# One plan of 730 named units orders a chain of sparse attention, channel mix and gated dense attention

## The chip, the cores and the metric

The kernel runs on one core of a Trainium2 chip. The metric is the time of one execution in device microseconds (us); of several executions the median is taken. TensorE is called PE here, VectorE DVE, ScalarE ACT, GpSimd POOL and SyncE SP, as the profile names them.

## The reference

Three stages in a row, on a batch of 4 with 576 positions:

```python
# stage 1: q, k, v are (4, 8, 576, 64); heads 0-3 local, heads 4-7 strided
scores = scale * np.matmul(q, k.transpose(0, 1, 3, 2))
mask_local = (rel >= 0) & (rel < 32)
mask_strided = (rel >= 0) & (pos[None, :] % 32 == pos[:, None] % 32)
x = softmax(where(mask, scores)) @ v            # to (4, 576, 512)
# stage 2: x_prev is x moved by one position
xk = mu_k * x + (1.0 - mu_k) * x_prev
xr = mu_r * x + (1.0 - mu_r) * x_prev
k = np.maximum(xk @ w_k, 0.0)                   # 512 -> 1024
x = sigmoid(xr @ w_r) * (k * k @ w_v)
# stage 3: four experts of width 64, causal, the two best by x @ w_gate
for e in range(4):
    q, k, v = x @ wq[e], x @ wk[e], x @ wv[e]
    ye = softmax(causal(scale * (q @ k.transpose(0, 2, 1)))) @ v @ wo[e]
    out += weight_of_e_if_among_the_two_best * ye
```

wq and wk are scaled up by 200. In the kernel most matrices are split into a high and a low fp32r part, and a product is three matmuls (high by high, low by high, high by low).

## The kernel before, in words

The kernel does not write its instructions down in the order in which the engines run them. A `Recorder` (line 187) stands in for the engines. Each operation recorded gets a rank (`len(self.ops)` at that moment) and a cost for each engine that could do it; matmuls that follow each other in one tiling of the array form one operation, until `cut()` closes it. At the end `order()` (line 357) lays the operations out in a modelled time: among those that one engine could start within `NEAR` (0.10 us) of the earliest, it takes the one of lowest rank. A PE operation that would change the tiling of the array has `stay` added to its rank (15 in stages 1 and 2, 10 in stage 3). `copy` may run on ACT or DVE, whichever would end first; most copies out of PSUM are such. `warm()` (line 346) puts matmuls on a tile of zeros ahead of a PE operation where the model has a gap of over 0.35 us in the first 80. `give()` issues everything (line 452, which is therefore the line of nearly every row of the trace), and `pinned()` fixes the order of each engine.

So the order of recording is the plan. It has these parts:

- Stage 1 of a batch (`p1_units`): per pair of heads a load, then pieces (three local thirds or two strided groups). Each piece is scores (`sl` local, `ss` strided, two heads side by side on halves of the array), softmax (`el`, `es`, on DVE and ACT), transposes (`ptl`, `pts`), their copies (`aTl`, `aTs`), the product with v (`pol`, `pos`) and its copy into `xT`.
- Stage 2 (`p2_units`): chunks A (320 positions) and Z (256). `r` and `k` are the token shift, `g` the product with w_r (`pr`), `m` with w_k (`pk`, then relu and square), `v` with w_v (`pv`, times the sigmoid, stored to `x_spill`). In the first batch a few products run on unsplit inputs (`xw`).
- Weights of stage 2 come in pieces: a load into `wraw`, a high part (`w`), a low part (`P`). `w3_units` does it for stage 3.
- Stage 3: `proj_units` gives q, k (`pq_False`, `pq_True`), v and the gate (`pvv`). Half of each K is copied to the other 64 partitions, its high part KH and low part KL by a DMA each that POOL issues. `attn_tiles` gives, for each of five tiles of queries, scores (`s`), softmax, transposes (`pt`), value products (`py`, a small tiling: 64 columns of the array) and the output product (`pw`), with a copy to `ot` and a store.

Before, the plan is made by rules. `first_batch()` runs the strings of `PLAN`: a head, written by hand, for the beginning, and a list that `interleave()` mixes with stage 1 of batch 1 by costs and a lead (0.9). `in_order` and `interleave` mix stage 2 of one batch with stage 1 of the next (0.85). In stage 3 the tiles form a pipeline with lags: scores of tile i, transposes of i - 1, py of i - 2, pw of i - 3 at one step, mixed with the projections of the next batch (0.85).

```python
def interleave(main, side, rec=None, lead=1.0):
    tm = lead * sum(c for c, _ in main) or 1.0
...
        if is_ < len(side) and (im >= len(main) or as_ / ts_ <= am / tm):
...
for i in range(b * per, len(steps) + 3 * last):
    for lag in range(4):
        if 0 <= i - lag < len(steps):
```

Of the kernel before, what the change touches and what calls it, by code (L numbers as in the profile page):

```python
# [9 lines left out]
F32 = mybir.dt.float32  # L10
# [8 lines left out]
P = 128  # L19
BIG = 3.0e38  # L20
PLAN = (
    "L1q L0q ident L0v L1v S3 L2q L3q zero L3v L0 L1 L2v L0m L1m L2 L3 L4 L5 L6 L7 L8 L9 L10 L11 L12 S4 S0 L13 W1 S1 S6 L14 S7 L15 W2 S9 Ar0 S8 Ar1 W0 W5 Ar2 W3 S5 S2 Ag0 Ag1 Ar3 Zr0 Zr2 Ak0 W6 Ak1 L16 W7 Zr3 Ak3 W4 L17 Ag2 Ak2 Am0 W9 L18 Zr1 W15 W11 W8 Am1 Age W10 Am2 W12 W16",
    "W13 Zg1 Am3 W14 Am4 Zg0 Zg3 L19 Zg2 Am5 Am6 W17 Am7 P8 W19 P15 P2 W18 P14 Zk0 P12 sig P13 Av0 P7 P10 P19 P17 P16 P18 P11 P6 Av1 Av2 Zk1 Av3 Av4 Zk3 P4 Zk2 Av5 P5 Av6 P9 Zm0 Zm1 Zm2 Zm3 Zm4 Av7 P1 Zm5 Zm6 Zm7 Zv0 Zv1 Zv2 Zv3 Zv4 Zv5 P0 Zv6 Zv7 P3",
)
# [12 lines left out]

def interleave(main, side, rec=None, lead=1.0):

    tm = lead * sum(c for c, _ in main) or 1.0  # L40
    ts_ = sum(c for c, _ in side) or 1.0
    im = is_ = 0
    am = as_ = 0.0
    while im < len(main) or is_ < len(side):
        if is_ < len(side) and (im >= len(main) or as_ / ts_ <= am / tm):
            c, f = side[is_]
            if rec is not None:
                rec.cut()
            f()
            as_ += c  # L50
            is_ += 1
        else:
            c, f = main[im]
            if rec is not None:
                rec.cut()
            f()
            am += c
            im += 1
# [92 lines left out]
class LazyPool:  # L151
    def __init__(self, make, bufs, psum=False, after=()):
        self.make, self.bufs, self.psum, self.after = make, bufs, psum, after
        self.made, self.rows, self.left = None, {}, 0
# [6 lines left out]
    def tile(self, shape, dtype, tag=None, name=None, bufs=None, lane=None, most=0):  # L161
        t = LazyTile(self, list(shape), dtype, bufs, dict(tag=tag, name=name))
        t.lane, t.most = lane, most
        t.row = self.rows.setdefault(tag, Row())
        t.row.free = [0.0] * (bufs or self.bufs)
        t.row.append(t)
        cols = np.arange(t.width).reshape(shape[1:])
        return View(t, (), dtype, 0, shape[0], cols)


def dram_view(ap):

# [14 lines left out]
class Recorder:  # L187
# [8 lines left out]
    STAY = 0  # L196
# [4 lines left out]
    def __init__(self, nc):  # L201
        self.nc = nc
        self.ops, self.on, self.open, self.more = [], False, None, []
        for e in self.ENGINES:
            setattr(self, e, self._engine(e))
# [32 lines left out]

    def add(self, ways, a, k):
# [9 lines left out]
        if mode is None or op is None or op.mode != mode:  # L249
            op = Op()  # L250
            op.stay = self.STAY
# [105 lines left out]
    def order(self):  # L357
# [43 lines left out]
        while len(given) < len(ops):  # L401
# [55 lines left out]
def kernel(  # L457
# [39 lines left out]
    def lazy(stack, name, bufs, after=(), before=None, **kw):  # L497
# [4 lines left out]
        return LazyPool(make, bufs, psum="space" in kw, after=after)  # L502
# [39 lines left out]
    nc.STAY = STAY1  # L542

    nc.zeros = p1.tile([P, P], F32, tag="zeros", name="zeros", bufs=1)
    nc.zeros.at = 1.6
# [115 lines left out]
    def p1_units(b):  # L661
        units = []
        xT = p2.tile([P, NKC, S + 1], F32, tag="xT", name=f"xT{b}", bufs=2)
        xTs[b] = xT

        def zero():
            nc.gpsimd.memset(xT[:, :, 0:1], 0.0)

        units.append((0.1, zero))
# [7 lines left out]
        def pair(hp):  # L677
# [56 lines left out]
            loads.append([(0.1, load), (0.0, load_rest)] + [(0.0, load_more)] * (b == 0 and local))  # L734

            def local_third(hf):
# [38 lines left out]
                def av_f():  # L775
# [11 lines left out]
                    evac(xT[:, hp, 1 + n * hf:1 + n * hf + n], po[:, :n])  # L787

                return (0.9, 0.4, 0.6), (sc_f, ex_f, no_f, tr_f, av_f)

            def strided_group(gi):
# [35 lines left out]
                def av_f():  # L827
# [10 lines left out]
                    xv = xT[:, hp, 1:].rearrange("p (n s) -> p n s", s=32)[:, :, r0:r0 + ng * nr]  # L838
# [5 lines left out]
                return (1.2, 0.6, 0.9), (sc_f, ex_f, no_f, tr_f, av_f)  # L844
# [6 lines left out]
        if b == 0:  # L851
            return units, loads, [f for _, f in stages]
        stages = [
            ((cs, lambda f=f: (f[0](), f[1](), f[2]())), (ct, f[3]), (ca, f[4]))
            for (cs, ct, ca), f in stages
        ]
        units += loads[0] + loads[1]
        groups = ((0, 1, 2), (3, 4, 5), (6, 7), (8, 9))
        for g in range(len(groups) + 1):
            if g in (1, 2):  # L860
                units += loads[g + 1]
            for n, i in ((1, g - 1), (2, g - 1), (0, g)):
                if 0 <= i < len(groups):
                    part = [stages[j][n] for j in groups[i]]
                    units.append((sum(c for c, _ in part), lambda part=part: [f() for _, f in part]))
        return units

    def p2_units(b):
        xT = xTs[b]
        parts = []  # L870
        for ci, (s0, N) in enumerate(CHUNKS1):
            st = {}

            def prep(which, kc, ci=ci, s0=s0, N=N, st=st):
                def f():
# [8 lines left out]
                    cur = xT[:, kc, 1 + s0:1 + s0 + N]  # L884
                    prv = xT[:, kc, s0:s0 + N]
# [14 lines left out]
                return (0.0, f)  # L900
# [4 lines left out]
            def mm1(fc, ci=ci, N=N, st=st):  # L905
# [28 lines left out]
                return (1.5 * N / 288, f)  # L934
# [18 lines left out]
            def mm3(oc, ci=ci, s0=s0, N=N, st=st):  # L953
# [14 lines left out]
                return (1.5 * N / 288, f)  # L968
# [4 lines left out]
            def mm2(oc, ci=ci, s0=s0, N=N, st=st):  # L973
                def half(hf):
# [19 lines left out]
                    return (1.5 * N / 288, f)  # L994
# [5 lines left out]
    def in_order(parts):  # L1000
        A, Z = parts
        return A["r"] + A["k"] + A["3"] + Z["r"] + A["1"] + Z["k"] + Z["3"] + A["2"] + Z["1"] + Z["2"]
# [19 lines left out]
    def first_batch():  # L1022

        (zero,), loads, steps = p1_units(0)
        A, Z = p2_units(0)
        pieces = weight_pieces()
        every = range(NKC)

        nc.vector.memset(nc.zeros, 0.0)
        todo = {"ident": [lambda: nc.sync.dma_start(ident, c_ident)], "zero": [zero[1]]}  # L1030
        for hp, l in enumerate(loads):
            for n, (_, f) in zip("qvm", l):
                todo[f"L{hp}{n}"] = [f]
        for i, step in enumerate(steps):
            todo[f"S{i}"] = step
        for j, (l, w, p) in enumerate(pieces):
            todo[f"L{j}"], todo[f"W{j}"], todo[f"P{j}"] = [l], [w], [p]
        for n, U in (("A", A), ("Z", Z)):
            for kc in every:
                todo[f"{n}r{kc}"], todo[f"{n}k{kc}"] = [U["r"][kc][1]], [U["k"][kc][1]]  # L1040
            for fc in range(NFC):
                todo[f"{n}m{fc}"] = [U["1"][fc][1]]
            for i, (_, f) in enumerate(U["2"]):
                todo[f"{n}v{i}"] = [f]
        for n, kcs in enumerate(((0, 1), (2,), (3,))):
            todo[f"Ag{n}"] = [lambda oc=oc, kcs=kcs: A["g"](oc, kcs) for oc in every]
        todo["Age"] = [lambda oc=oc: A["ge"](oc) for oc in every]
        for oc in every:
            todo[f"Zg{oc}"] = [lambda oc=oc: Z["g"](oc, every), lambda oc=oc: Z["ge"](oc)]
        todo["sig"] = [lambda: nc.scalar.activation(sg, sg, AF.Sigmoid)]  # L1050

        def run(name):
            for f in todo[name]:
                nc.cut()
                f()

        head, rest = (p.split() for p in PLAN)
        for name in head:
            run(name)
        cost = {"A": 1.6, "Z": 1.3}  # L1060
        return [(cost[n[0]] if n[1] in "mv" and n[0] in cost else 0.5 if n[0] == "P" else 0.0, lambda n=n: run(n)) for n in rest]

    def mixed(units, others):
        res = []
        interleave([(1.0, lambda u=u: res.append(u)) for u in units], [(1.0, lambda u=u: res.append(u)) for u in others])
        return res
# [16 lines left out]
    def w3_units():  # L1083

        units = []
        for src, h, l in ((wq, wqh, wql), (wk, wkkh, wkkl), (wvg, wvgh, wvgl), (wo, woh, wol)):
# [8 lines left out]
            units.append((0.0, load))  # L1095
            for r in range(0, rows, rows // 2):
# [5 lines left out]
                units.append((1.0, part))  # L1102
        return units

    A, Z = p2_units(B - 1)
    main = in_order((A, Z))
    n = len(main) - len(A["2"] + Z["1"] + Z["2"])
    interleave(main[:n], [], nc)
    interleave(main[n:], w3_units(), nc)
# [3 lines left out]
    nc.sync.dma_start(mcau, c_cau)  # L1113

# [426 lines left out]
```

## Time and profile before

| what | us |
|---|---|
| median of 3 runs (lowest, highest) | 525.83 (524.87, 526.89) |
| the profiled execution | 525.04 |
| its span, first to last instruction | 523.3 |
| PE busy | 518.0 (99%), 4360 instructions |
| DVE busy | 367.3 (70%), 1318 instructions |
| ACT busy | 314.4 (60%), 929 instructions |
| mean granted clock of TensorE | 0.999 of full |

In a row of the timeline the first number is the start in the span, the second the time from there to the end of the row's last instruction. Matmuls overlap, so the price of one is read from start to start of neighbours, not from its duration. A matmul of plain float32 operands (not split ones) has two records in the trace, so counts there are twice those of the order. A row's brackets give the idle time ahead of it on its engine, and what ended it.

### The profile page before, as it was taken

What the parts mean: (1) busy time and instruction counts of PE and PEld (TensorE: products, weight loads), DVE (VectorE), ACT (ScalarE), POOL (GpSimd) and SP (SyncE); (2) the same over time, 40 slices, a digit from 0 to 9 for tenths busy, and PEclk for the clock granted to TensorE, in tenths of its full rate; (3) what the DMA queues carried; (4) which work ended last, traced back from release to release, by engine and by line L of the source; (5) the groups of instructions that cost most, each with busy time, mean ns of one, the idle gap of its engine ahead of it and who ended that gap; (6) DMA issues with size and microseconds to landing.
All of it is one profiled execution on the core that took longest, in us unless ns stands there. A gap on an engine that the chain in (4) does not pass through costs nothing.

```text
span 523.3 us, 11666 instructions
## 1 busy us (share of the span) xinstructions
PE 518.0 (99%) x4360; PEld 483.1 (92%) x4360; DVE 367.3 (70%) x1318; ACT 314.4 (60%) x929; POOL 37.8 (7%) x88
## 2 busy tenths in 40 slices
PE   9999999999999999999999999999999999999997
PEld 8767799999999999999999999999999998998886
DVE  3999999639773758674747733266999768766991
ACT  4999985727673825664734553144765555666664
POOL 0000000000000000000000000033232030211000
PEclk9999999999999999999999999999999999999999
DMA  8997022221203330203021230055233330312112
GB/s 263 366 414 292 1 96 85 105 63 71 72 1 110 106 122 11 73 2 108 14 61 61 83 112 30 31 144 131 63 95 78 106 90 3 90 32 67 51 43 90
DMA packets 28892, 50.22 MB, mean 96 GB/s; under 512 B 4900, under 2 KB 23332, under 8 KB 28068
## 3 DMA queue, kind: packets, MB, share of 16 engines
q1 hardware_dynamic: 23716, 44.76, 25.0%
q0 software_dynamic: 5120, 4.72, 4.4%
q8 instruction: 34, 0.56, 0.4%
q14 instruction: 22, 0.18, 0.1%
HBM read 35.18 MB, written 9.44 MB: 85 GB/s over the span
## 4 chain that ended last, share of the span: by engine, by line
PE 96%; DVE 2%; ACT 0%; issue 0%; ACTq 0%
PE pk L452 20%; PE pv L452 20%; PE pr L452 10%; PE s L452 6%; PE pvv L452 5%; PE pw L452 5%; PE pq_False L452 5%; PE pq_True L452 5%; PE pt L452 5%; PE py L452 5%; PE sl L452 3%; PE pol L452 2%; PE ss L452 2%; PE ptl L452 2%; PE pos L452 1%; PE pts L452 1%
## 5 line engine op out<-in xcount | busy, mean ns | idle before, releaser
L452 PE MATMUL pv<-kk,wvh 128*128 128x320 f32 (+1 forms) x512 | 104.0, 297 | 0.0
L452 PEld LDWEIGHTS pv<-kk,wvh 128*128 128x128 f32 x512 | 81.2, 188 | 1.1
L452 PE MATMUL pk<-xh,wkh 128*128 128x256 f32 (+1 forms) x224 | 67.3, 300 | 0.0
L452 PE MATMUL pk<-xl,wkh 128*128 128x256 f32 (+1 forms) x224 | 65.3, 292 | 0.0
L452 ACT ACTIVATE rf<-pk 128x320 f32<-128x320 f32 (+1 forms) x64 | 25.5, 406 | 42.2 <-PE pk L452 41.8
L452 ACT ACTIVATE pe<-pe,nm 128x384 f32<-128x384 f32 (+4 forms) x72 | 41.8, 583 | 14.2 <-DVE nm L452 12.2
L452 DVE TENSOR_TENSOR sg<-pv,sg 128x320 f32<-128x320 f32 (+1 forms) x32 | 14.6, 456 | 42.2 <-PE pv L452 41.9
L452 PEld LDWEIGHTS pk<-xh,wkh 128*128 128x128 f32 x224 | 42.1, 188 | 1.1
L452 PEld LDWEIGHTS pk<-xl,wkh 128*128 128x128 f32 x224 | 42.1, 188 | 0.0
L452 DVE CUSTOM_DVE_ANT_0 pe<-s,mcau 128x384 f32<-128x384 f32 (+4 forms) x72 | 32.6, 483 | 6.4 <-PE s L452 6.1
L452 ACT ACTIVATE es<-es,nm 108x108 f32<-108x108 f32 (+1 forms) x80 | 30.4, 383 | 5.3 <-DVE nm L452 5.1
L452 ACT ACTIVATE el<-el,nm 128x96 f32<-128x96 f32 x72 | 26.1, 364 | 6.6 <-DVE nm L452 6.2
L452 DVE CAST kk<-rf 128x320 fp32r<-128x320 f32 (+1 forms) x51 | 15.7, 309 | 20.2 <-ACT rf L452 19.9
L452 DVE TENSOR_TENSOR kk<-rf,kk 128x320 fp32r<-128x320 f32 (+1 forms) x64 | 28.8, 456 | 1.6 <-ACT kk L452 0.4
L452 PE MATMUL pt<-ident,pe 128*128 128x128 f32 x200 | 29.8, 276 | 0.0
L452 ACT ACTIVATE rf<-rf 128x320 f32<-128x320 f32 (+1 forms) x64 | 28.0, 445 | 1.2
L452 PE MATMUL pr<-xh,wrh 128*128 128x320 f32 (+1 forms) x96 | 28.7, 299 | 0.0
L452 PE MATMUL pr<-xl,wrh 128*128 128x320 f32 (+1 forms) x96 | 28.2, 294 | 0.0
L452 DVE SCALAR_TENSOR_TENSOR xf<-xd,mu,xT 128x256 f32<-128x256 f32 (+1 forms) x52 | 25.7, 510 | 0.2
L452 DVE TENSOR_SCALAR pe<-pe,sm 128x384 f32<-128x384 f32 (+4 forms) x72 | 25.2, 397 | 0.4
L452 PEld LDWEIGHTS pt<-ident,pe 128*128 128x128 f32 x200 | 23.0, 140 | 2.2 <-ACT aT L452 0.3
L452 PE MATMUL py<-aT,V 128*64 128x320 f32 (+4 forms) x224 | 24.6, 362 | 0.0
(291 smaller groups left out, 1562.2 us busy)
## 6 DMA issues: line engine op xcount, KB each, us to landing
qkv<-in_loc_dram SPq DMA_DIRECT2D x6, 1168.0 KB, 5.4
qkv<-in_strd_dram SPq DMA_DIRECT2D x6, 896.0 KB, 4.9
wraw<-in_w_k_dram SPq DMA_DIRECT2D x8, 512.0 KB, 9.8
wraw<-in_w_v_dram SPq DMA_DIRECT2D x8, 512.0 KB, 10.2
x_spill<-sg SPq DMA_DIRECT2D x16, 160.0 KB, 1.7
x2f<-x_spill SPq DMA_DIRECT2D x4, 640.0 KB, 4.6
out_dram<-ot SPq DMA_DIRECT2D x16, 160.0 KB, 1.8
wraw<-in_w_r_dram SPq DMA_DIRECT2D x4, 512.0 KB, 7.5
```

Of the source, the lines that this page charges most:

```text
L452: f[o.engine](*[now(x) for x in a], **{n: now(x) for n, x in k.items()})
```

## The change

`PLAN` is one string of 730 names. The digit is the batch. In stage 1, `L` is a load (`q`, `v`, `m` its parts), `S` scores and softmax of a piece, `T` its transposes, `V` its product with v. `L`, `W`, `P` with a number are also pieces of the weights in the first batch. `A` and `Z` with `r`, `k`, `g`, `m`, `v` are stage 2. `u`, `x`, `k`, `q`, `v`, `t`, `g`, `n` are the projections of stage 3, `s` scores, `m` the norm, `p` transposes, `a` the value products, `o` the output products. `Recorder.unit` takes a unit's name and function, `Recorder.run` records the units as the plan names them; `interleave`, `first_batch`, `in_order` and the lags are gone. The ordering of the recorded operations (`order()`) stays, but for constants of its model: when zeros are there, and how DMAs of SP land. Batches 2 and 3 of stages 1 and 2 stand nearly in the regular order of before; the first batch (with batch 1 and a part of 2 among it) and stage 3 are reshuffled. The tile `xT` of a batch is made in its unit `z`.

```diff
-PLAN = (
-    "L1q L0q ident L0v L1v S3 L2q L3q zero L3v L0 L1 L2v L0m L1m L2 L3 L4 L5 L6 L7 L8 L9 L10 L11 L12 S4 S0 L13 W1 S1 S6 L14 S7 L15 W2 S9 Ar0 S8 Ar1 W0 W5 Ar2 W3 S5 S2 Ag0 Ag1 Ar3 Zr0 Zr2 Ak0 W6 Ak1 L16 W7 Zr3 Ak3 W4 L17
...
+PLAN = """
+0L1q 0z 0L0q 0i 0L2q 0L1v 0S3 0L0 0S4 0T3 0V3 0L3q 0L3v 0L1 0L0v 0L0m 0L2v 0S1 0L1m 0W1 0W0 0T4 0S0 0L2 0S6 0T1 0L3
...
+3a10 3p12 3a11 3a00 3a01 3o11 3o13 3o03 3o00 3o12 3o10 3o01 3o02
+"""
...
-LATE = True
-STAY3 = 10
...
-STAY1 = 15
-LEAD0 = 0.9
-LEAD1 = 0.85
-LEAD2 = 0.85
...
+    def unit(self, name, f):
+
+        assert name not in self.units, name
+        self.units[name] = f, self.stay
+
+    def run(self, plan):
+        for self.token in plan.split():
+            f, self.stay = self.units.pop(self.token)
+            self.cut()
+            f()
+        assert not self.units, self.units
...
-                link = max(link, s + (1.6 if s < 8 else 1.9))
-                link += o.lag[e] / (0.24 if link < 8 else 0.38)
+                link = max(link, s + (1.2 if s < 1 else 1.6 if s < 8 else 2.0))
+                link += o.lag[e] / (0.24 if link < 8 else 0.37)
...
-    nc.zeros.at = 1.6
+    nc.zeros.at = 2.7
...
+        for i, f in enumerate(stages):
+            nc.unit(f"{b}S{i}", lambda f=f: several(*f[:3]))
+            nc.unit(f"{b}T{i}", f[3])
+            nc.unit(f"{b}V{i}", f[4])
...
-    interleave(first_batch(), p1_units(1), nc, LEAD0)
-    for b in range(1, B - 1):
-        interleave(in_order(p2_units(b)), p1_units(b + 1), nc, LEAD1)
...
+            for ep in range(EP):
+                nc.unit(f"{b}a{ci}{ep}", av(ep))
+            for oc in range(NKC):
+                nc.unit(f"{b}o{ci}{oc}", wout(oc))
...
-    nc.STAY = STAY3
-    interleave(proj_units(0), [], nc)
...
+        proj_units(b)
+        attn_units(b)
+    nc.vector.memset(nc.zeros, 0.0)
+    nc.run(PLAN)
```

**The end of the last batch's attention, on PE.** `pt` are transposes, `py` value products (chunk, pair of experts; one py is 10 or 4 rows of matmuls), `pw` output products. Before:

```order
L452 MATMUL pt_3_0_1_6917<-ident,pe_0_1_6844 128x128
L452 MATMUL py_1_1_6920<-aT_3_1_1_6742,V_6297 64x320 x6
...
L452 MATMUL pt_3_0_2_6944<-ident,pe_0_2_6848 128x128
...
L452 MATMUL pt_3_1_3_6963<-ident,pe_1_3_6904 128x128 x2
L452 MATMUL py_0_0_6968<-aT_3_0_0_6934,V_6297 64x256 x2
...
L452 MATMUL py_0_1_6974<-aT_3_0_1_6955,V_6297 64x256 x2
...
L452 MATMUL pw_1_0_6981<-yh_1_6931,woh 128x320
```

and in the change:

```order
L467 MATMUL pt_3_1_2_6923<-ident,pe_1_2_6774 128x128 x2
L467 MATMUL py_1_0_6928<-aT_3_1_0_6720,V_6335 64x320 x6
...
L467 MATMUL py_1_1_6942<-aT_3_1_1_6709,V_6335 64x320 x6
...
L467 MATMUL py_0_0_6957<-aT_3_0_0_6865,V_6335 64x256 x2
...
L467 MATMUL py_0_1_6963<-aT_3_0_1_6901,V_6335 64x256 x2
...
L467 MATMUL pw_1_1_6971<-yh_1_6953,woh 128x320
```

The four value products, which stood in three visits to the small tiling with transposes between, now stand in one.

**The first loads, on SP.** `qkv_0` and `qkv_1` are the two pairs of local heads, `qkv_2` and `qkv_3` the strided ones (1152 columns are q and k, 768 or 640 are v); `mstr` is the strided mask. Before:

```order
L452 DMA ident<-in_c_ident_dram 128x128
L452 DMA qkv_0_77<-in_loc_dram 128x768
L452 DMA qkv_1_72<-in_loc_dram 128x768
L452 DMA mstr_111<-in_c_str_dram 126x126
L452 DMA mstr_120<-in_c_str_dram 108x108
L452 DMA mu<-in_mu_dram 128x8
L452 DMA qkv_2_136<-in_strd_dram 128x1152
L452 DMA qkv_3_150<-in_strd_dram 128x1152
```

and in the change:

```order
L467 DMA ident<-in_c_ident_dram 128x128
L467 DMA qkv_2_97<-in_strd_dram 128x1152
L467 DMA qkv_1_72<-in_loc_dram 128x768
L467 DMA mstr_107<-in_c_str_dram 126x126
L467 DMA mstr_113<-in_c_str_dram 108x108
L467 DMA mu<-in_mu_dram 128x8
L467 DMA wraw<-in_w_r_dram 128x1024
L467 DMA qkv_3_148<-in_strd_dram 128x1152
```

The q and k of the first strided pair went ahead of five loads, and one pair's local v (qkv_0) went behind the weights of w_r.

**The first matmuls, on PE**, zeros among them (each row of zeros is named after the tile that is computed next). Before:

```order
L452 MATMUL sl_1_0_87<-zeros 128x64 x9
L452 MATMUL sl_1_0_87<-qkv_1_72 64x96 x6
...
L452 MATMUL ptl_1_0_164<-zeros 128x64 x3
L452 MATMUL ptl_1_0_164<-ident,el_1_0_122 96x128 x3
L452 MATMUL ptl_1_1_182<-zeros 128x64
L452 MATMUL ptl_1_1_182<-ident,el_1_1_131 96x128 x3
L452 MATMUL pol_1_0_192<-aTl_1_0_177,qkv_1_72 64x64 x6
...
L452 MATMUL ss_2_0_0_225<-qkv_2_136 126x126
```

and in the change:

```order
L467 MATMUL sl_1_0_86<-zeros 128x64 x4
L467 MATMUL sl_1_0_86<-qkv_1_72 64x96 x6
...
L467 MATMUL sl_0_1_125<-zeros 128x64 x2
L467 MATMUL sl_0_1_125<-qkv_0_77 64x96 x6
...
L467 MATMUL ptl_1_0_161<-zeros 128x64
L467 MATMUL ptl_1_0_161<-ident,el_1_0_109 96x128 x3
...
L467 MATMUL ss_2_0_0_186<-qkv_2_97 126x126
...
L467 MATMUL pol_1_0_198<-aTl_1_0_171,qkv_1_72 64x64 x6
```

Of the nine zeros ahead of the first scores four are left, two more stand ahead of a later score, and the first strided scores (`ss`) stand ahead of the first `pol`.

## Rows read from the trace of the kernel before

**Rows 1.** Windows: length, busy us of PE, PEld, DVE, ACT, POOL, clock, DMA share, GB/s.

```profile
6.36:14.25 7.89, 7.67 (x93) 6.74 (x91) 5.44 (x36) 6.16 (x29) 0.00 (x0) 1.00 1.01 358
14.25:39.15 24.90, 24.19 (x225) 17.89 (x222) 24.58 (x105) 23.78 (x84) 0.21 (x1) 1.00 1.02 391
39.15:500.00 460.85, 460.85 (x3856) 436.12 (x3855) 326.61 (x1135) 270.63 (x776) 37.29 (x82) 1.00 0.25 76
```

**Rows 2.** The timeline of PE at the start: start, duration, engine, operation, count.

```profile
1.05 4.10 PE L452 MATMUL sl<-zeros 128*128 128x64 f32 x18 [1.05 <-DVE zeros L452]
5.09 4.11 PE L452 MATMUL sl<-qkv 64*64 64x96 f32 x48
...
10.39 0.49 PE L452 MATMUL ptl<-ident,el 128*96 128x128 f32 x3
...
20.32 1.21 PE L452 MATMUL sl<-qkv 64*64 64x96 f32 x24
...
27.17 0.81 PE L452 MATMUL pr<-xw,w('r', 0)_458 128*128 128x320 f32 x2 [0.23 <-DVE w('r', 0)_458 L452]
...
39.15 0.70 PE L452 MATMUL pk<-xw,w('k', 0, 0)_596 128*128 128x320 f32 x2
```

**Rows 3.** The timeline of PE in the attention, py alone and joined.

```profile
390.91 2.27 PE L452 MATMUL py<-aT,V 128*64 128x320 f32 x20
393.12 0.44 PE L452 MATMUL pt<-ident,pe 128*128 128x128 f32 x2
...
480.84 0.34 PE L452 MATMUL s<-KH,Q 128*128 128x384 f32 x1
481.02 0.34 PE L452 MATMUL s<-KL,Q 128*128 128x384 f32 x1
481.29 4.33 PE L452 MATMUL py<-aT,V 128*64 128x320 f32 x40
485.55 0.44 PE L452 MATMUL pt<-ident,pe 128*128 128x128 f32 x2
```

**Rows 4.** The timeline of PE in stage 2, small tilings side by side.

```profile
69.00 0.57 PE L452 MATMUL pol<-aTl,qkv 96*64 96x64 f32 x12
69.50 1.70 PE L452 MATMUL sl<-qkv 64*64 64x96 f32 x36
...
81.11 0.92 PE L452 MATMUL pol<-aTl,qkv 96*64 96x64 f32 x24
81.96 0.49 PE L452 MATMUL ss<-qkv 64*126 64x126 f32 x4
```

**Rows 5.** The timeline of DVE ahead of the first pk, its copies that move.

```profile
18.37 0.73 DVE L452 COPY aTs<-pts 126x252 f32<-126x252 f32 x2
...
36.50 0.55 DVE L452 COPY aTl<-ptl 96x384 f32<-96x384 f32 x1
...
38.62 0.36 DVE L452 COPY xT<-pol 128x192 f32<-128x192 f32 x1 [0.17 <-PE pol L452]
```

**Rows 6.** The timeline of PE, transposes among full-array matmuls.

```profile
440.78 0.44 PE L452 MATMUL pt<-ident,pe 128*128 128x128 f32 x2
440.97 0.36 PE L452 MATMUL pq_True<-x2h,wkkh 128*128 128x256 f32 x1
...
445.30 0.60 PE L452 MATMUL pt<-ident,pe 128*128 128x128 f32 x4
445.65 0.39 PE L452 MATMUL pw<-yh,woh 128*128 128x320 f32 x1
```

**Rows 7.** Copies of K: timelines of ACT and POOL, DMA issues, waits of POOL.

```profile
416.79 0.69 ACT L452 CAST KH<-pq_True 128x640 fp32r<-128x640 f32 x1 [0.18 <-PE pq_True L452]
...
419.44 0.51 POOL L452 DMA_DIRECT2D KL<-KL  x1
...
KL<-KL POOLq DMA_DIRECT2D x4, 80.0 KB, 2.2
...
POOL KH L452 <- DMA KH<-KH: 27.4, 16, 3.1
```

More of the change, by code (lines that the diff above doesn't have):

```diff
@@ L850, in p1_units, with several @@
             pair(hp)
[L851 to L866, printed above, removed]
+        def several(*fs):
+            for f in fs:
+                nc.cut()
+                f()
+        for hp, l in enumerate(loads):
+            if b == 0:
+                for n, f in zip("qvm", l):
+                    nc.unit(f"0L{hp}{n}", f)
+            else:
+                nc.unit(f"{b}L{hp}", lambda l=l: several(*l))
+        for i, f in enumerate(stages):
+            nc.unit(f"{b}S{i}", lambda f=f: several(*f[:3]))
+            nc.unit(f"{b}T{i}", f[3])
+            nc.unit(f"{b}V{i}", f[4])
     def p2_units(b):
-        xT = xTs[b]
         parts = []
@@ L1020, in pinned @@
             prev[i.engine] = i
[L1022 to L1053, printed above, removed]
-                nc.cut()
[L1055 to L1066, printed above, removed]
-    interleave(first_batch(), p1_units(1), nc, LEAD0)
-    for b in range(1, B - 1):
-        interleave(in_order(p2_units(b)), p1_units(b + 1), nc, LEAD1)
+    p1_units(0)
+    A, Z = p2_units(0)
+    every = range(NKC)
+    nc.unit("0i", lambda: nc.sync.dma_start(ident, c_ident))
+    for j, parts in enumerate(weight_pieces()):
+        for n, f in zip("LWP", parts):
+            nc.unit(f"0{n}{j}", f)
@@ new lines, with gates, gate @@
+    for n, kcs in enumerate(((0, 1), (2,), (3,))):
+        def gates(kcs=kcs):
+            for oc in every:
+                nc.cut()
+                A["g"](oc, kcs)
+        nc.unit(f"0Ag{n}", gates)
+    nc.unit("0Age", lambda: [A["ge"](oc) for oc in every])
+    for oc in every:
+        def gate(oc=oc):
+            Z["g"](oc, every)
+            Z["ge"](oc)
+        nc.unit(f"0Zg{oc}", gate)
+    nc.unit("0sig", lambda: nc.scalar.activation(sg, sg, AF.Sigmoid))
+    for b in range(1, B):
+        p1_units(b)
+        p2_units(b)
@@ L1313, in f @@
                         )
-                    return (0.4, f)
-                return [sc(e) for e in range(E)], [(0.0, norm)] + [trp(e) for e in range(E)]
+                    return f
+                nc.unit(f"{b}m{t}", norm)
+                for e in range(E):
+                    nc.unit(f"{b}s{t}{e}", sc(e))
+                    nc.unit(f"{b}p{t}{e}", trp(e))
             def tail_units(s0=s0, probs=probs):
@@ L1373, in f @@
                             )
[L1374 to L1376 removed]
+                    return f
+                nc.unit(f"{b}m{t}", norm)
+                for e in range(EP):
+                    nc.unit(f"{b}s{t}{e}", sc(e))
+                    nc.unit(f"{b}p{t}{e}", trp(e))
             def av(ep, ci=ci, s0=s0, N=N, cst=cst, tiles=tiles):
```

196 lines of the change are left out of this document (90 added, 106 removed).

## The prediction

> **What bounds the kernel now.** I read the table of windows first, because the program has three regimes. From 39.15 us to 500 us TensorE (PE) is busy for 460.85 of 460.85 us, while VectorE (DVE) is busy for 326.61 and ScalarE (ACT) for 270.63 [rows 1]. No wait of PE stands in that stretch, so a better order of the other engines buys nothing there: only what PE itself spends on its sequence can shrink. Ahead of 39.15 it is different. Between 14.25 and 39.15 us DVE is busy for 24.58 of 24.90 us and ACT for 23.78, and PE's 24.19 contain matmuls on the tile of zeros, which compute nothing [rows 1, 2]. There DVE, with ACT close behind, sets when the dense work can begin. Between 6.36 and 14.25 us DVE stands idle for 7.89 - 5.44 = 2.45 us and ACT for 7.89 - 6.16 = 1.73 [rows 1]. Then I read PE's own list of the start. It shows when the first matmul of the dense stage 2 that multiplies by w_k begins (pk, 39.15), and where zeros are multiplied [rows 2].
>
> That start cuts the program in two. By the order of the rows, the same real matmuls stand ahead of the first pk in both kernels, and the same ones behind it. So the change of time is the change of that start, plus what changes behind it, where PE is saturated and each saved change of its array's tiling counts in full.
>
> **The change part by part.** The number of real instructions is the same on PE. What moves is the order; the zeros are fewer (24 rows before, 14 now), and nine PSUM copies go from ACT to DVE.
>
> *Changes of tiling.* I counted them in PE's order behind the first pk. A visit is a leave from full-array matmuls into small tiles (sl, ss, pol, pos, py) and back: 37 visits before (24 in stages 1 and 2, 13 in the attention), 24 now (18 and 6). Changes from one small tiling straight to another go from 12 to 17. The price of a visit comes from py. Alone, 20 py and the return take 393.12 - 390.91 = 2.21 us, so two visits take 4.42. Joined, 40 py and one return take 485.55 - 481.29 = 4.26 [rows 3]. The difference, 0.16, is one way out. The way in: the last s ahead of py takes 481.29 - 481.02 = 0.27 us instead of the 0.18 that s of this width takes from start to start (480.84 to 481.02), so 0.09 [rows 3]. A visit costs 0.25 us, and 13 fewer give 13 x 0.25 = -3.2. For small to small: 12 pol and the change to sl take 0.50 us (69.00 to 69.50), 24 pol and the change to ss take 0.85 (81.11 to 81.96) [rows 4]. So 12 pol are 0.35 and the change is 0.15; five more cost +0.75. Sum of this term: **-2.4**. Bounds: if a change from small to small costs as much as a whole visit, 5 x 0.25 leaves -2.0; if such a change costs nothing, -3.2; if only the way out is saved, 13 x 0.16 less 0.75, -1.3.
>
> *The start.* By DVE's order ahead of the first pk, two copies aTs (the second row of the pair begins with 0.73 us for both) and one copy aTl (0.55) leave DVE, and one copy xT (0.36) comes [rows 5]: -0.73 - 0.55 + 0.36 = -0.92 us of work on the engine that sets the start. ACT takes the three copies and gives others away, two casts of weights among them, about +0.5 in the sum, which is less than its idle time. Besides, the plan fills DVE's hole: SP now issues the q and k of the strided heads ahead of the v of the local ones, and PE multiplies the first strided scores ahead of the first pol. Of the 2.45 us [rows 1] I take nearly half, 0.9, because ACT has only 1.73 + (24.90 - 23.78) = 2.85 us of its own to give in the same stretch and each link of this chain crosses it. Term: **-1.8**, so the first pk at about 37.3. Bounds: 0, if ACT or the weights' transfers (the DMA share is 1.02 there [rows 1]) set it; -0.92 - 2.45 = -3.4, if all of the hole is filled.
>
> *Behind the start, on DVE.* It is 99% busy ahead of 39.15 [rows 1] and has copies to do that were ACT's. The weights' low parts for pk are needed in the order in which PE takes them, and the change runs seven pk in a row early. By DVE's order the last part is ready about 3 us ahead of its use, so I cost this at nothing; if that cover is gone, it takes back the start's gain (first rival).
>
> *Transposes among matmuls.* Groups of transposes (pt) between dense matmuls are more: 144 changes for 114. Both use the full array. Two pt take 0.19 us from start to start (440.78 to 440.97), four take 0.35 (445.30 to 445.65) [rows 6]: 0.08 each and 0.03 a group. I take 0, since the 0.03 lies near what one row can tell; the bound is 30 x 0.03 = +0.9.
>
> *Copies of K.* Half of each projected K goes to the other half of the partitions by DMAs from GpSimd (POOL). After the projection the chain is the cast (from 416.79), the low part, two issues one after the other (the second at 419.44, 0.51 long), and 2.2 us to landing: 419.44 + 0.51 + 2.2 - 416.79 = 5.4 us [rows 7]. In the plan the shortest stretch of PE work between a projection of K and its first scores is about 5.7 us (last batch; 8.2 before, the shortest), an estimate: the sum of what the matmuls that stand between take from start to start in this trace. Term 0, with 0.3 us to spare. Bound: POOL's waits for an earlier copy go up to 3.1 us [rows 7], so +3.
>
> *The end.* Eight pw stand at the end in both, the last 256 wide. 0.
>
> Sum: -2.4 - 1.8 = -4.2. On the profiled execution, 525.04 us, that gives 520.8. The median of the three runs is 525.83, 0.79 above it, and the next runs will scatter about that: 525.8 - 4.2 = **521.6 us**.
>
> **A rule against the rows: the clock at the start.** Rows first. The 48 sl at 5.09 take 4.11 us, 0.086 each; the 24 sl at 20.32 take 1.21, 0.050 each, 1.7 times faster [rows 2]. So TensorE runs at the lower of its two levels (1.2 GHz) until about 10.4 us and at the upper one (2.4 GHz) after it (the column of the granted clock reads 1.00 over the whole window [rows 1], so the durations are what shows it), though the zeros run without a gap from 1.05 to 5.09. The change issues only 4 rows of zeros there instead of 9; at 4.10 / 18 = 0.23 us for each of their two passes, they end near 2.9, and PE may stand bare for some 2 us. *The Trainium skill, "TensorE: Matmul & The Clock Gate", Part 1, says that the throttled state is the default, that activity releases it and idleness brings it back: by it fewer zeros could mean a later rise.* *The trace here agrees that the lower level comes first, but not that unbroken zeros alone release it.* I take no delay, since the sl and the first transposes that precede the rise stand there in both kernels; the other case is the third rival.
>
> **The rivals.**
> *The start does not move* (or DVE gives the gain back behind it). For it: DMA share 1.02 and an ACT that is 96% busy [rows 1]. Against it: a hole of 2.45 us on DVE, and less work for DVE. 525.8 - 2.4 = 523.4 us. Chance 0.18.
> *The whole hole is filled*: 525.8 - 2.4 - 3.4 = 520.0. Against it: ACT. Chance 0.12.
> *Slower: the clock rises late.* Between 10.39 and 27.17 us (the first pr) lie 16.8 us, of which 24 passes of zeros at 0.23 / 1.7 = 0.13 us [rows 2] and the idle 0.71 [rows 1] are 3.9; the other 12.9 us of matmuls at 0.086 / 0.050 = 1.72 times their price cost +9.3, less the 3.9 that zeros and idleness gave up, +5.4. Then 525.8 - 2.4 + 5.4 = 528.8. It becomes slower than before once the start loses over 2.4 us, which needs the rise to come after about 22 us. Chance 0.07.
> *K's copies late*: two of eight wait 1.5 us, or one 3: 525.8 - 4.2 + 3 = 524.6. Chance 0.08.
> *The plan does not do what it says*, since batches 2 and 3 keep nearly their old order and the saved visits hide something I don't see: 525.8. Chance 0.05.
> The forecast has 0.50.
>
> **How the numbers follow.** What a measurement of this kernel can tell from no change is about 0.5%, 2.6 us: faster means under 523.2. The forecast (0.50) and the filled hole (0.12) are faster: 0.62. Start unmoved, K late and no effect are within: 0.31. The late clock is slower: 0.07. The range: down to 519.0, which holds the filled hole and one more microsecond for the bounds of the visits; up to 525.0, which holds the unmoved start and the late K, and leaves out the late clock and the plan without effect (0.12).
>
> **What would show it.** Right: the first pk near 37.3 us; from there to the last pw PE without a wait and 2.4 us shorter, with py in groups of 40 and more where 20 stood; the lower level ends near 10.4 us again. Wrong: a first pk at 39 or later; sl at 0.08 us each in rows after 12 us; a wait of PE for KH or KL, or for w('k') just behind the first pk; or a dense stretch that keeps its length though the visits are gone.

## The result, and the profile after

The change takes 519.05 us (median of 5, 518.66 to 519.21), the kernel before 525.81 us (5 runs, 524.87 to 526.89): ratio 0.987, 95% interval 0.9856 to 0.9883. So it is faster by 6.8 us, where 4.2 were forecast; 519.05 lies at the very edge of the range (519.0 to 525.0). The profiled execution of the change is 519.05 us with a span of 517.3, that of before 525.04 with 523.3. Inside the two spans 6.0 us went; the other 0.8 is that the profiled execution of before ran 0.8 under its median.

First the windows of the change, cut at its own first pk (columns as in [rows 1]):

```profile
6.36:14.25 7.89, 7.50 (x79) 6.30 (x80) 5.34 (x39) 6.05 (x31) 0.00 (x0) 1.00 0.98 363
14.25:37.42 23.17, 22.20 (x215) 16.30 (x213) 23.10 (x95) 22.64 (x83) 0.11 (x1) 1.00 1.02 390
37.42:500.00 462.58, 462.48 (x3901) 440.31 (x3900) 334.16 (x1177) 277.98 (x795) 37.25 (x82) 1.00 0.25 77
```

The regimes are those of [rows 1]: PE is full behind the first pk (462.48 of 462.58), DVE nearly so ahead of it (23.10 of 23.17 from 14.25 us on). Then PE's timeline, at the places of [rows 2] and [rows 3]:

```profile
1.05 1.97 PE L467 MATMUL sl<-zeros 128*128 128x64 f32 x8 [1.05 <-DVE zeros L467]
3.85 2.18 PE L467 MATMUL sl<-qkv 64*64 64x96 f32 x24 [0.83 <-DMA qkv<-in_loc_dram]
...
11.02 0.84 PE L467 MATMUL ptl<-ident,el 128*96 128x128 f32 x3
...
12.93 0.53 PE L467 MATMUL ptl<-ident,el 128*96 128x128 f32 x3
...
37.42 0.70 PE L467 MATMUL pk<-xw,w('k', 0, 0)_567 128*128 128x320 f32 x2
...
336.78 0.28 PE L467 MATMUL pq_True<-x2h,wkkh 128*128 128x256 f32 x1
...
501.75 5.63 PE L467 MATMUL py<-aT,V 128*64 128x320 f32 x56
507.31 0.41 PE L467 MATMUL pw<-yh,woh 128*128 128x320 f32 x1
507.56 0.31 PE L467 MATMUL pw<-yl,woh 128*128 128x320 f32 x1
507.71 0.31 PE L467 MATMUL pw<-yh,wol 128*128 128x320 f32 x1
...
513.68 0.28 PE L467 MATMUL pw<-yh,wol 128*128 128x256 f32 x1
```

The three boundaries to read are the first pk, the first pq_True (stage 3 begins) and the last pw. In the kernel before the first pk is at 39.15 [rows 2], and the other two are these:

```profile
340.08 0.28 PE L452 MATMUL pq_True<-x2h,wkkh 128*128 128x256 f32 x1
...
519.68 0.28 PE L452 MATMUL pw<-yh,wol 128*128 128x256 f32 x1
```

| stretch | before | change | difference | forecast |
|---|---|---|---|---|
| start, to the first pk | 39.15 | 37.42 | -1.73 | -1.8 |
| stage 2, first pk to first pq_True | 300.93 | 299.36 | -1.57 | -0.75 |
| attention, first pq_True to last pw | 179.60 | 176.90 | -2.70 | -1.75 |
| behind the last pw | 3.6 | 3.6 | 0 | 0 |

(The forecast's -2.4 behind the start, -2.5 before rounding, is -0.75 for 6 visits and 5 small changes, and -1.75 for 7 visits.) In these two executions the start came out as forecast; the dense stretches won 0.8 and 0.95 us more. PE waits for only 0.10 us in them, so what they won must lie in the matmuls' own sequence.

### The profile page after: what moved, and what is told of

The parts are those of the page before. It is cut to its first block, busy times and chain, and to the rows that moved or that the text cites. A ratio compares the mean times of both kernels' runs of the same rounds, so it can differ in the third digit from the quotient of the medians.

```text
span 517.3 us, 11621 instructions
## 1 busy us (share of the span) xinstructions
PE 510.6 (99%) x4340; PEld 478.5 (93%) x4340; DVE 366.1 (71%) x1322; ACT 314.6 (61%) x925; POOL 37.7 (7%) x88
## 4 chain that ended last, share of the span: by engine, by line
PE 95%; DVE 2%; DMA 1%; SPq 0%; issue 0%; ACT 0%; ACTq 0%; DVEq 0%
PE pk L467 21%; PE pv L467 20%; PE pr L467 10%; PE s L467 6%; PE pvv L467 5%; PE pw L467 5%; PE pq_True L467 5%; PE pq_False L467 5%; PE pt L467 4%; PE py L467 4%; PE sl L467 2%; PE ss L467 2%; PE pol L467 2%; PE ptl L467 2%; PE pos L467 2%; PE pts L467 1%
## 5 line engine op out<-in xcount | busy, mean ns | idle before, releaser
L467 ACT ACTIVATE pe<-pe,nm 128x128 f32<-128x128 f32 (+4 forms) x72 | 41.9, 582 | 16.1 <-DVE nm L467 8.3
L467 DVE CAST kk<-rf 128x256 fp32r<-128x256 f32 (+1 forms) x45 | 13.8, 306 | 25.6 <-ACT rf L467 18.4
L467 ACT COPY aT<-pt 128x512 f32<-128x512 f32 (+3 forms) x51 | 22.4, 459 | 5.4 <-PE pt L467 5.1
L467 ACT COPY sg<-pr 128x320 f32<-128x320 f32 (+1 forms) x31 | 12.3, 400 | 20.7 <-PE pr L467 20.5
```

The source lines that it names most:

```text
L467: f[o.engine](*[now(x) for x in a], **{n: now(x) for n, x in k.items()})
```

## The experiments

The same three boundaries were read in the trace of every run. The trace is of one execution; the time is the median of all executions of that run ("one" where there was only one):

| run | first pk | stage 2 | attention | time, us |
|---|---|---|---|---|
| change | 37.42 | 299.36 | 176.90 | 519.05 |
| old attention | 38.13 | 299.38 | 179.56 | 521.37 |
| old stages 1 and 2 | 39.43 | 300.81 | 177.35 | 522.49 |
| stay 0 | 39.39 | 304.59 | 176.90 | 523.98 |
| 32 visits of 2 | 37.12 | 317.78 | 176.90 | 537.18 (one) |
| 32 visits of 6 | 37.47 | 332.73 | 176.92 | 552.50 (one) |
| old order of loads | 41.05 | 301.48 | 176.93 | 525.53 |
| no zeros | 38.73 | 299.40 | 176.91 | 519.83 |
| more zeros | 37.78 | 299.38 | 176.91 | 519.39 |
| transposes by 2 | 37.25 | 306.54 | 176.94 | 526.76 (one) |
| transposes by 4 | 36.98 | 306.40 | 176.89 | 526.21 (one) |
| new loads alone | 39.02 | 301.14 | 179.60 | 525.52 |
| narrow, single | 36.82 | 302.88 | 176.91 | 521.99 (one) |
| narrow, in pairs | 37.58 | 302.18 | 179.49 | 524.62 (one) |

Where the order of PE is the same, a dense stretch has the same length within 0.04 us (299.36 to 299.40), so it can be read far finer than the whole time. The last run's attention is the exception, told below.

The start is another matter. Nine of these traces have, ahead of the first pk, the same instructions in the same order on every engine, zeros included, and yet their first pk lies between 36.82 and 39.39 us. It goes with the moment at which TensorE goes from its lower level (1.2 GHz) to its upper one (2.4 GHz), which the durations of the small matmuls show (the trace's first record of the granted clock stands at the same moment):

| run | lower level ends, us | first pk | idle time of DVE ahead of it |
|---|---|---|---|
| transposes by 2 | 7.5 | 37.25 | 8.09 |
| 32 visits of 2 | 8.0 | 37.12 | 8.01 |
| narrow, single | 10.0 | 36.82 | 7.39 |
| transposes by 4 | 10.3 | 36.98 | 7.63 |
| change | 11.7 | 37.42 | 8.07 |
| 32 visits of 6 | 12.1 | 37.47 | 8.07 |
| narrow, in pairs | 12.6 | 37.58 | 8.16 |
| old attention | 13.5 | 38.13 | 8.64 |
| stay 0 | 17.1 | 39.39 | 9.89 |

The rows of the two ends, transposes by 2 and stay 0:

```profile
1.06 1.97 PE L480 MATMUL sl<-zeros 128*128 128x64 f32 x8 [1.06 <-DVE zeros L480]
...
7.05 1.39 PE L480 MATMUL sl<-qkv 64*64 64x96 f32 x24
...
8.74 0.51 PE L480 MATMUL ptl<-ident,el 128*96 128x128 f32 x3
```

```profile
1.06 1.97 PE L466 MATMUL sl<-zeros 128*128 128x64 f32 x8 [1.06 <-DVE zeros L466]
...
7.30 2.19 PE L466 MATMUL sl<-qkv 64*64 64x96 f32 x24 [0.18 <-DMA qkv<-in_loc_dram]
...
13.62 0.88 PE L466 MATMUL ptl<-ident,el 128*96 128x128 f32 x3
...
16.61 0.75 PE L466 MATMUL ptl<-ident,el 128*96 128x128 f32 x3
```

Between 10 and 17 us each microsecond of a later rise puts the first pk back by about 0.36 us ((39.39 - 36.82) / (17.1 - 10.0)). DVE's work is the same in all nine (29.1 to 29.5 us); it is its idle time that grows, while PE's small matmuls that feed it take longer (0.88 us for three transposes instead of 0.51). A rise ahead of 10 us gains nothing more: in the first run PE then waits for loads (1.1 us for the strided ones, 0.9 for local v). No run shows what makes the rise early or late. So a first pk from a single trace can be off by a microsecond or two.

**The two halves, each undone.** The old order was written as unit names, from the rules of the kernel before. Only the names behind `mc`, or those ahead of it, are exchanged; the constants of the model stay those of the change. With the old attention, PE and DVE have there exactly the order of before. With the old stages 1 and 2 the order is not quite that of before (20 rows of zeros instead of 24, and some copies on other engines). A piece of the attention:

```diff
-0s40 1v1 0s41 1x1 1k10 0s10 0m3 1q10 1k11 0s11 0p31 0p33
+0s40 1v1 0s41 1x1 1k10 0m3 0p30 0p31 0p32 0p33 0s00 1q10
```

and, for stages 1 and 2, from the first name on:

```diff
-0L1q 0z 0L0q 0i 0L2q 0L1v 0S3 0L0 0S4
+0L1q 0z 0L0q 0i 0L0v 0L1v 0S3 0T3 0V3
```

> The new plan up to the masks, the old order of the attention behind it (13 visits to the small tiling instead of 6). Theory A, a visit costs more than I priced (0.32 us, because the pair of matmuls behind it is slow too): the attention takes 179.6 us again instead of 176.9, the whole 519.05 + 2.7 = 521.7 us; start and stage 2 stay as in the change (first pk at 37.4). Theory B, a visit costs 0.25 us and what was won beyond that comes from other stalls of the reshuffled program: 7 x 0.25 = +1.75, so 520.8, or anything up to 521.7 with stalls of PE that can be named.

> The old order of stages 1 and 2 (with the first batch and its loads), the new attention. Both theories: the start goes back to about 39.1 us (+1.7) and stage 2 to 300.9 us (+1.6), the attention stays at 176.9: 519.05 + 3.3 = 522.3 us. If the start and the dense parts depend on each other (a late start that hides behind something), the sum of this run's loss and that of the run with the old attention is not the whole difference of 6.8 us.

With the old attention the time is 521.37 us (ratio to before 0.9928, 0.9912 to 0.9945), and the attention takes 179.56 us: all 2.7 back, stage 2 untouched. With the old stages 1 and 2 it is 522.49 us (0.9959, 0.9942 to 0.9976), start and stage 2 are as before, and the attention takes 177.35. By the ratios the halves win 0.7% and 0.4%, together 1.1% of the 1.3% +- 0.13: they add up within their intervals. This places the gain, and doesn't yet say why it is larger than priced.

**More visits by the planner.**

```diff
-    STAY = 15
+    STAY = 0
```

> The change, with the stay of stages 1 and 2 at 0 instead of 15: PE's order goes to the small tilings and back 36 times behind the first pk instead of 18, and changes between small tilings 10 times instead of 17. Theory A (0.32 us a visit, 0.13 a change between small tilings): stage 2 from 299.4 us to 299.4 + 18 x 0.32 - 7 x 0.13 = 304.2. Theory B (0.25 and 0.15): 299.4 + 4.5 - 1.05 = 302.8. The start as in the change; the whole about 523.9 by A and 522.5 by B.

Stage 2 is 304.59 us, +5.23 against the 4.85 that theory A gives and the 3.45 of B. (The whole, 523.98 us, is 4.93 above the change, as A has it. The trace is of the slowest of the ten executions, 526.24 us, the one with the late clock in the table above; its start of 39.39 is not due to the edit, which leaves every engine's order ahead of the first pk as it was.)

**The price of a visit by itself.** Small matmuls are put ahead of a group's first matmul, two in one run and six (`* 6`) in the other; `self.small` is the tile `ident`.

```diff
+    def poke(self, o):
+        t = next((t for t in o.tiles if t.pool.psum and not t.opened), None)
+        if t is None or not (o.token or "").startswith(("3A", "3Z")):
+            return
+        out = View(t, (), F32, 0, P, np.arange(t.width))[:64, :64]
+        f = dict(tensor=self.nc.tensor.matmul)
+        v = self.small
+        o.calls[:0] = [(f, (out, v[:, :64], v[:, :64]), dict(start=True, stop=True))] * 2
...
             if e == "tensor":
+                self.poke(o)
```

> The change, with two matmuls of 64 columns on the small tiling put ahead of the first matmul of each of 32 groups of the last batch's dense stage 2 (they write the group's tile, which the group then overwrites): 32 visits more, and nothing else. Four passes of about 0.03 us each are 0.12 us. Theory A: 32 x (0.32 + 0.12) = +14.1 us, and the rows show 0.09 ahead, 0.13 behind and 0.10 more between the first two dense matmuls. Theory B: 32 x (0.25 + 0.12) = +11.8 us, with no slow second matmul.

> As the run with two small matmuls a visit, with six: 32 visits again, eight passes more in each. Both theories: 32 x 8 x 0.03 = +7.7 us over that run; if the price of a visit depends on how long PE stays in it, it is something else. The visit's own price is what is left when the passes are taken off both runs.

Stage 2 is longer by 18.42 us with two, and by 14.95 more with six. Eight passes in 32 visits are 256, so a pass is 0.058 us. (That is twice my 0.03, because the two halves of a pol go side by side: in the trace of before two pol start 0.007 us apart, and the next two 0.058 later.) Then 18.42 / 32 - 4 x 0.058 = **0.342 us** a visit. PE's timeline of the run with two shows where it goes:

```profile
298.42 0.31 PE L477 MATMUL pk<-xl,wkh 128*128 128x320 f32 x1
298.56 0.31 PE L477 MATMUL pk<-xh,wl('k', 3, 1)_992 128*128 128x320 f32 x1
298.80 0.45 PE L477 MATMUL pk<-ident 128*64 128x64 f32 x4
299.18 0.42 PE L477 MATMUL pk<-xh,wkh 128*128 128x320 f32 x1
299.43 0.31 PE L477 MATMUL pk<-xl,wkh 128*128 128x320 f32 x1
299.58 0.31 PE L477 MATMUL pk<-xh,wl('k', 0, 1)_1076 128*128 128x320 f32 x1
```

From start to start: 0.24 on the way in, where 0.147 is usual (+0.09); 0.38 for four passes of 0.058 (+0.15); and then 0.25 between the first two dense matmuls, where 0.147 is usual (+0.10). My two terms are the first two. The third I had not counted, though it stood in the kernel before, behind every visit that dense matmuls follow: 71.13 to 71.52 for two pv there, where the next two take 0.29.

```profile
71.13 0.55 PE L452 MATMUL pv<-kk,wvh 128*128 128x320 f32 x2
71.52 0.31 PE L452 MATMUL pv<-kk,wl('v', 0)_855 128*128 128x320 f32 x1
71.67 0.46 PE L452 MATMUL pv<-kk,wvh 128*128 128x320 f32 x2
71.96 0.31 PE L452 MATMUL pv<-kk,wl('v', 1)_871 128*128 128x320 f32 x1
```

In [rows 3] it can't be seen, because two transposes stand behind py, and I ended the measure at the first of them. With 0.34 for a visit, stay 0 should have shown 18 x 0.34 - 7 x 0.13 = 5.2 us; it showed 5.23.

**The start: the order of loads.** `0L2q` behind `0S3` and `0L0v` ahead of `0L1v`, as before; and the reverse edit in the old order.

```diff
-0L1q 0z 0L0q 0i 0L2q 0L1v 0S3 0L0 0S4
+0L1q 0z 0L0q 0i 0L0v 0L1v 0S3 0L2q 0L0 0S4
```

> The change, with the plan's first names moved so that SP loads in the old order (q and k of the first strided pair behind the local v). Theory A, the start moved because DVE's early hole was filled: DVE is idle again for some 2.4 us between 6 and 14 us and the first pk comes 0.5 to 1.5 us later than 37.42. Theory B, only the 0.92 us of copies taken off DVE did it: the first pk within 0.3 us of 37.42 whatever DVE idles early. Three more visits stand behind the first pk in this order (21 for 18), +0.9, so the whole is 520.5 to 521.5 by A and 519.6 to 520.2 by B.

> The order of before with one thing of the change: q and k of the first strided pair are named, and so loaded, ahead of the local v. Theory A: the start's gain is due to DVE getting strided work into its early hole, which needs these loads: the first pk at 38.3 or earlier (1 us of the 1.7), stage 2 and the attention as before: 524.8 us. Theory B: the loads help only together with the new order of the pieces behind them, so the first pk stays at 39.1 to 39.5 or comes later: 525.8 or more.

With the old loads in the new plan the first pk is at 41.05, and the time is 525.53 us (ratio 1.0016, 0.9985 to 1.0046): nearly all is lost, more than either theory gave. With the new loads alone in the old order the first pk is at 39.02 and the time 525.52 us (0.9995, 0.9976 to 1.0013): nothing is won, as theory B has it. This run, too, has the constants of the change, so ahead of the first pk its pair is the run with the old stages 1 and 2, which differs there in the loads alone. The windows from the start to the first pk say why; the third busy time is DVE's, the fourth ACT's. Before, the change, the old loads in the new plan, the new loads in the old order, the old loads in the old order:

```profile
0.00:39.15 39.15, 37.17 (x342) 29.82 (x343) 30.18 (x141) 31.22 (x114) 0.52 (x6) 1.00 0.95 347
```

```profile
0.00:37.42 37.42, 34.18 (x322) 26.69 (x323) 29.35 (x140) 30.42 (x115) 0.41 (x6) 1.00 0.94 344
```

```profile
0.00:41.05 41.05, 37.08 (x338) 28.94 (x339) 32.34 (x147) 30.22 (x110) 0.41 (x6) 1.00 0.96 359
```

```profile
0.00:39.02 39.02, 34.53 (x338) 27.18 (x338) 30.97 (x145) 30.10 (x109) 0.41 (x6) 1.00 0.94 346
```

```profile
0.00:39.43 39.43, 35.41 (x334) 28.10 (x335) 30.14 (x141) 31.46 (x115) 0.51 (x6) 1.00 0.94 340
```

DVE's idle time is 8.97, 8.07, 8.71, 8.05 and 9.29 us. In the old order, too, it is shorter with the new loads, by 1.24 us, as theory A says (the clock rose 2.3 us earlier in that trace, at 6.8 for 9.1 us, so this need not be the loads alone). But the planner, with other loads, gives DVE other copies: its work is 30.18, 29.35, 32.34, 30.97 and 30.14 us. Old loads in the new plan put 3.0 us of work on DVE (the clock rises there at 11.8 us, as in the change); new loads in the old order 0.8, which takes most of the gain away. The start is the sum of both. The other 2.1 us that the old loads cost stand in stage 2 (301.48): three more visits are 1.0 of them and a wait of PE for DVE's `xT` 0.4; the rest has no name.

**The zeros and the clock.**

```diff
-    WARM, FILL, IDLE = 80.0, 0.8, 0.35
+    WARM, FILL, IDLE = 0.0, 0.8, 0.35
```

> The change without any matmul on zeros. Theory A, the zeros have nothing to do with when TensorE goes from the lower to the upper level: rise near 10.4 us as before, the first pk within 0.3 us of 37.42, 519 us. Theory B, the zeros bring the rise forward: without them the small matmuls run at the lower level (sl at 0.086 us instead of 0.050) for some us more, the first pk up to 5 us later, up to 524 us.

For more zeros, `nc.zeros.at` is 1.6 again instead of 2.7.

> The change with the model's time of the zeros as it was before (1.6 instead of 2.7): some more zeros ahead of the first scores, 18 rows for 14. Theory A, zeros don't matter: 519.0 us. Theory B, they bring the rise forward: the rise earlier than in the change and the first pk up to 1 us earlier, 518.

Without zeros the time is 519.83 us (ratio 0.9886, 0.9859 to 0.9912). In the trace three transposes still take 0.87 us at 15.84, and the upper level begins at about 16.7 us; PE also stands bare ahead of its scores:

```profile
7.03 2.18 PE L466 MATMUL sl<-qkv 64*64 64x96 f32 x24 [1.00 <-DMA qkv<-in_loc_dram]
9.14 1.78 PE L466 MATMUL ptl<-ident,el 128*96 128x128 f32 x6
...
15.84 0.87 PE L466 MATMUL ptl<-ident,el 128*96 128x128 f32 x3
...
18.04 0.62 PE L466 MATMUL pts<-ident,es 126*126 126x126 f32 x4
```

In the change the upper level begins at about 11.7 us (0.84 for three transposes at 11.02, 0.53 at 12.93, above). The granted-clock column reads 1.00 from 6.36 us in the change too, so durations have to be read. By these two traces theory B would hold for the clock. But stay 0, with all the zeros of the change, rises at 17.1, later than the run without any, and transposes by 2 rises at 7.5. One trace without zeros, inside that scatter, shows neither that the zeros bring the rise forward nor that they don't. Its first pk, 38.73, lies between those of old attention and stay 0, as its rise does, and the whole time can't be told from the change's. With four more rows of zeros (519.39 us, 0.9879, 0.9857 to 0.9901) the first pk is at 37.78 and the rise at 11.3, both within the scatter: no difference.

**Transposes in small groups.** As in the runs on visits, with transposes of `ident` onto the whole array: two ahead of each group, or four (`* 4`) ahead of every second one.

```diff
+        out = View(t, (), F32, 0, P, np.arange(t.width))[:, :P]
+        f = dict(tensor=self.nc.tensor.transpose)
+        o.calls[:0] = [(f, (out, self.small, self.small), dict())] * 2
```

> The change, with two full-array transposes of a 128 x 128 tile put ahead of the first matmul of each of the 32 groups of the last batch's dense stage 2 (64 in all; the group overwrites what they write). Read with the next run, which has the same 64 in 16 groups of four. Theory A: a group of transposes among dense matmuls costs nothing (in the rows the matmul behind starts 0.08 us early and holds up the next by as much), so stage 2 is as long in both within 0.1 us, about 299.4 + 64 x 2 x 0.11 = 313.4 us. Theory B: a group costs 0.03 us, my bound: 0.5 us longer here. Theory C: a group gains 0.05 us and more, and so the extra groups of the change explain part of what it won in the attention: 0.8 us shorter here.

> As the run with two transposes ahead of each group, with four ahead of every second one: 64 again, in 16 groups. Stage 2: the same by A, 0.5 us shorter than with 32 groups by B, 0.8 us longer by C.

Stage 2 takes 306.54 and 306.40 us: sixteen more groups cost 0.14, 0.009 each. That is theory A but for 0.04; the bound of 0.03 and the gain are both excluded. (A transpose took 7.18 / 64 = 0.112 us; my sum of 313.4 had it twice.)

**Narrow matmuls.** The last open part of the attention. `w` and `x` are those of the group's own first matmul.

```diff
+        f, (out, w, x), k = o.calls[0]
+        o.calls[:0] = [(f, (out[:, :P], w, x[:, :P]), dict(start=True, stop=True))] * 1
```

> The change, with one fp32r matmul of 128 columns put ahead of each of the 32 groups of the last batch's dense stage 2 (256 or 320 columns; the group overwrites what it writes): 32 narrow matmuls, each between wide ones. Read with the next run, which has the same 32 in 16 pairs. Theory A: a narrow matmul between wide ones takes 0.06 us, and behind another narrow one 0.11, so spreading them saves about 0.05 each: stage 2 is 299.4 + 32 x 0.06 = 301.3 us here. Theory B: it takes 0.11 wherever it stands and what the trace shows at the scores is put back right behind: 299.4 + 32 x 0.11 = 302.9 us here and there.

> As the run with one narrow matmul ahead of each group, with two ahead of every second one. Theory A: 299.4 + 16 x (0.06 + 0.11) = 302.1 us of stage 2, 0.8 longer than with them spread. Theory B: 302.9 us, the same as spread.

Stage 2 takes 302.88 and 302.18 us: a single narrow matmul costs 3.52 / 32 = 0.11 us, one of a pair 0.088. Theory A falls: to spread them saves nothing.

The second run shows something else. Its attention, with the same order as in the change, takes 179.49 us, because PE waited for the copies of K in the first batch:

```profile
PE s L479 <- DMA KL<-KL: 2.3, 2, 1.3
```

On POOL's timeline of that stretch the second issue of KL waits 1.98 us for an earlier copy and comes at 363.37, 2.5 us after its KH:

```profile
360.88 0.51 POOL L479 DMA_DIRECT2D KH<-KH  x1 [1.21 <-DMA KH<-KH]
363.37 0.51 POOL L479 DMA_DIRECT2D KL<-KL  x1 [1.98 <-DMA KL<-KL]
```

It is one execution. One other trace, that with the old stages 1 and 2, has a little of it: an s on KL starts 0.37 us behind its s on KH, where 0.18 is usual, and 0.05 behind the landing of a copy of KL; its attention is 177.35.

```profile
365.84 0.33 PE L466 MATMUL s<-KH,Q 128*128 128x384 f32 x1
366.21 0.45 PE L466 MATMUL s<-KL,Q 128*128 128x384 f32 x1
```

In all the others the attention is within 0.05 us of 176.90 or 179.60.

## Why the prediction was right or wrong

**Right: what bounds the kernel, and the split.** Ahead of the first pk it is DVE's work and idle time; behind it PE's own sequence. No new wait came (PE full for 462.48 of 462.58 us), and the tail is the same.

**The start: the parts came as forecast in one pair of traces, and the closeness is luck.** It is -1.73 for -1.8. DVE's work fell by 30.18 - 29.35 = 0.83 us (forecast 0.92; 0.7 to 1.1 in the nine traces of this beginning). Its idle time fell by 0.90 (forecast 0.9), but that depends on the clock. The clock rose at 10.3 us in the trace of before and at 11.7 in that of the change; in the trace with the same beginning and a rise at 10.3 (transposes by 4) the first pk is at 36.98, which is -2.17, and DVE's idle time is 1.34 less. By the medians it would be about -2.5, an estimate: 6.76 less the 4.27 behind the start.

The gain's place was not quite as I put it, either. The windows of before, of the change and of the run with the old loads:

```profile
0.00:6.36 6.36, 5.30 (x34) 5.19 (x36) 0.17 (x1) 1.28 (x1) 0.31 (x5) 1.00 0.60 162
```

```profile
0.00:6.36 6.36, 4.48 (x34) 4.09 (x35) 0.91 (x10) 1.73 (x4) 0.31 (x5) 1.00 0.61 152
```

```profile
0.00:6.36 6.36, 4.50 (x34) 4.12 (x35) 1.09 (x10) 1.91 (x4) 0.31 (x5) 1.00 0.63 156
6.36:14.25 7.89, 7.37 (x78) 6.24 (x78) 4.49 (x28) 5.79 (x27) 0.00 (x0) 1.00 1.02 377
```

From 6.36 to 14.25 us DVE is busy for 5.34 us in the change, no more than the 5.44 of [rows 1]: the hole is not smaller. The first scores now begin at 3.85 instead of 5.09 us, since fewer zeros stand ahead of them, so local softmax moved out of the hole to the front (0.91 us of work ahead of 6.36 for 0.17), and strided work took its place (with the old loads the hole has 4.49).

**Wrong: the price of a visit.** This is the step that failed: "A visit costs 0.25 us, and 13 fewer give 13 x 0.25 = -3.2". The way in and the way out were right; the sum left out what a visit costs behind it. Measured by itself a visit is 0.34 where dense matmuls follow: +0.09 in, +0.15 out, and +0.10 that the pair behind it loses. Where transposes follow, the third part is 0.06 (two pt behind a py take 0.20 us to the next start, 485.55 to 485.75 in the kernel before; two among the transposes put in by hand take 0.14). Of the 4.27 us won behind the start, the edges of the seven fewer visits in the attention account for about 2.2 us (summed over the two traces; 7 x 0.32) and those of the six in stage 2 for 2.1 (6 x 0.34). The five changes from small to small took back some 0.7, for 0.75 forecast.

That 519.05 still fell inside the range is luck: its lower end was put at 519.0 for a filled hole, which did not come.

**Still open:** 2.2 + 2.1 - 0.7 = 3.6 of the 4.27. The remaining 0.7 us, most of it in the attention, lies in many differences of under 0.1 us each. It is not the groups of transposes (0.009 each) and not the spreading of narrow scores; I have no run that names it. (The bound of 0.9 on transposes was itself too wide: it took the 30 more changes as 30 groups, but a group has two changes, into it and out of it.)

**The rivals.** That the start doesn't move, or that the whole hole is filled, did not come. The late clock did not come in the change's profile, but it is real: with the same beginning it came once, in the run with stay 0, at 17.1 us, and the first pk came 2.4 us later than in the trace with a rise at 10.3. I had put a loss of 2.4 us at a rise after 22 us, because I let the zeros and PE's idle time give way first; the traces show DVE waiting instead. In the change the rise came 1.4 us later than in the trace of before, which, in a scatter of 7.5 to 17.1, tells nothing of the fewer zeros. *The Trainium skill has it that activity releases the throttled state ("TensorE: Matmul & The Clock Gate", Part 1).* *Every trace here agrees in so far as it begins at the lower level and reaches the upper one while PE works; what fewer zeros do to that moment no run here shows.* K's copies late: not in the change's profile, but once in an execution of the same attention, for 2.6 us, near the 3 that I had priced, and for part of 0.45 us in another. The plan's margin there is as thin as I had it.

## What to carry to other kernels

A change of mode has a price on both sides and a little behind: measure it from an undisturbed matmul before to an undisturbed one after, not to the first of the next kind, or put extra ones in a dense stretch and divide. Where one engine is full, count such changes first; they were worth about the same in stage 2 and in the attention (0.34 and 0.32 us). Where a planner assigns the copies, an edit of the loads is never only that: read the work and the idle time of the engine that sets the end, each by itself. And compare a stretch only between executions that agree in the granted clock: a median of ten and the trace of one of them can be 2 us apart.

## What the runs showed that I had not expected

- The pair of dense matmuls behind a visit takes 0.25 us instead of 0.147 from the first to the second, in every visit that dense matmuls of 320 columns follow (0.22 for 0.12 with 256).
- Moving one load and one of its neighbours back cost 6.5 us of the 6.8 won (by the medians), of which 3.6 at the start, through 3.0 us of copies that the planner then gave to DVE.
- A dense stretch repeats within 0.04 us from run to run, so a term of 0.01 us per group could be read from single executions. The start scatters by 2.6 us with not one instruction changed, and follows the moment at which the clock rises (7.5 to 17.1 us).
